# Weights split in two as they land, in place, and a first MLP tile in three passes: banded attention with a rational MLP on one core

## The chip, the core and the metric

One core of a Trainium2 chip runs the whole program. Its engines are TensorE (PE in the profile, its weight loads PEld), VectorE (DVE), ScalarE (ACT), GpSimd (POOL) and SyncE (SP), which here issues every DMA. The metric is the device time of one execution in microseconds (us), the median of three runs.

## The reference

Eight batches of eight heads attend over 576 positions within a window of 128, with a linear bias; the heads are laid side by side to a matrix x of 4608 x 512. Then comes an MLP with a rational activation:

```
scores = where(0 <= i-j < 128, q @ k.T / 8 - slope_h * |i-j|, -1e9)
x      = softmax(scores) @ v                   # 4608 x 512
h      = x @ w_in                              # 4608 x 2048
P      = a0 + a1*h + a2*h^2 + a3*h^3
Q      = 1 + |b0|*|h| + |b1|*h^2
out    = (P / (Q + 1e-6)) @ w_out              # 4608 x 512
```

The weights w_in and w_out are handed to the kernel as 64-bit floating-point numbers of two 32-bit words each.

## The kernel before

**Tiles.** x is cut into 36 blocks of 128 rows and the MLP into 17 tiles: tile 0 has three blocks, tiles 1 to 15 two each, tile 16 three. w_in and w_out are cut into 16 chunks of 128 columns or rows (`c`). For every tile and chunk, "up" (`up`, L625) makes h for the chunk in a PSUM buffer tagged `h` (three of them), ScalarE, GpSimd and VectorE turn it into g (L648 to L666), and "down" (`down`, L681) adds g times w_out into the accumulators `acc`. Tiles of two blocks take two chunks in one step (512 columns), tiles of three one chunk (384 columns). Tile 0's third accumulator takes one of the three `h` buffers.

**Two formats.** From tile 1 on every product is made in three passes of the fast format F32R: the high parts of both factors, high by low and low by high. So x, g and the weights exist as a high and a low part (`x_hi`/`x_lo`, `g_h`/`g_l`, `wi_hi` and `wo_hi`/`w_lo`). Tile 0 runs on whole F32 numbers (`w32`, `x_hi`, `g_32`), which PE does in one, slower, instruction sequence.

**Weights.** Each of the 32 half chunks k (even: w_in, odd: w_out) is loaded by one DMA of 512 KB into a tile `raw_w` and made into F32 by `convert`: GpSimd scales the top words (L582), ScalarE takes three bits of the low words into `cv` in PSUM (L583), and VectorE joins them with two instructions (L584, L585) into `w32`. The first 16 raw tiles have eight homes; of the later ones all even k share one buffer (`x_lo0`) and all odd k one other (`spare`). Later, in `split`, ScalarE rounds `w32` into the high part (L599) and VectorE or GpSimd subtracts it for the low part (L600), which goes to the memory of a `w32` no longer needed.

**Attention.** A unit (`attention`) is a pair of heads for two blocks: scores on PE (L463), masks and exponentials, a GpSimd product (L514), a transposition (L524), two more GpSimd products (L531, L532) and the values (L409). Twelve units belong to the start: six for tile 0, four for tile 1, two that run ahead.

**Order.** `Plan.order()` writes the order of every engine's instructions out by hand beforehand, from due times and costs in ns; the constants `A0` to `BL` set the due times. On the chip each engine then runs its list strictly in that order.

Of the kernel before, what the change touches and what calls it, by code (L numbers as in the profile page):

```python
# [784 lines left out]
```

## Time and profile before

| what | us |
|---|---|
| median of 3 runs (lowest to highest) | 1040.03 (1039.03 to 1040.55) |
| the profiled execution, whole time | 1040.95 |
| the profiled execution, span of the core | 1039.1 |
| PE busy in the span | 1001.4 |
| DVE, ACT, POOL busy | 795.0, 677.0, 524.3 |

The span runs from the first to the last instruction of the core. Busy is the time in which an engine has an instruction under way, waits within an instruction included. PE's clock is given as a share of 2.4 GHz.

### The profile page before, as it was taken

Reading aid. Unit: us, or ns where it says so; the run is one execution under the profiler, and the core shown is the slowest. Engines: PE = TensorE matmul, PEld = TensorE weight load, DVE = VectorE, ACT = ScalarE, POOL = GpSimd, SP = SyncE. Lnnn points to the kernel's source line nnn. Section 1 sums busy time; section 2 is a strip of 40 time slices with the busy share of each in tenths; the row PEclk is TensorE's granted clock in tenths of the full one; section 3 lists DMA queues with packets and bytes.
Section 4 is the critical chain, followed back from the end, with each engine's and each line's share of the span. In section 5 each row is a group of like instructions: output and inputs, shape, how many; then the busy total and the mean of one; then the engine's idle time right before and its main releaser. Section 6 shows DMA issues by size and latency. Waiting matters only on the chain.

```text
span 1039.1 us, 24386 instructions
## 1 busy us (share of the span) xinstructions
PE 1001.4 (96%) x9223; PEld 856.0 (82%) x9223; DVE 795.0 (77%) x1916; ACT 677.0 (65%) x1572; POOL 524.3 (50%) x570
## 2 busy tenths in 40 slices
PE   5899879999999999999999999999999999999998
PEld 4654447888898989898989888888889888898897
DVE  4798789877777777777777777777777786877776
ACT  3766767666766666766666666666665767676664
POOL 2854479455454445444445555545453635465332
PEclk7899999999999999999999999999999999999999
DMA  7945522020212121211212111212121212120000
GB/s 226 293 120 164 177 66 69 27 92 27 92 30 84 35 83 47 61 55 60 62 47 68 48 62 48 68 45 68 52 73 47 67 46 83 31 76 2 21 1 31
DMA packets 75894, 74.15 MB, mean 71 GB/s; under 512 B 7808, under 2 KB 60544, under 8 KB 75776
## 3 DMA queue, kind: packets, MB, share of 16 engines
q1 hardware_dynamic: 75776, 72.58, 22.8%
q8 instruction: 73, 1.20, 0.5%
q14 instruction: 45, 0.37, 0.1%
HBM read 63.11 MB, written 9.44 MB: 70 GB/s over the span
## 4 chain that ended last, share of the span: by engine, by line
PE 86%; DVE 4%; DMA 3%; ACT 2%; SPq 2%; POOL 2%; issue 1%; DVEq 0%; POOLq 0%; ACTq 0%
PE h L625 38%; PE acc L681 37%; PE sc L409 5%; PE sc L463 4%; PE pt L524 3%; DMA raw_w<-in_w_out 2%; SPq L384 1%; ACT o L709 1%; DVE w_lo L600 1%; DMA kq<-in_kqv 1%; DVE h L658 0%; POOL g_q L651 0%; DVE g_q L657 0%; DMA raw_w<-in_w_in 0%; DVE cv L584 0%
## 5 line engine op out<-in xcount | busy, mean ns | idle before, releaser
L625 PE MATMUL h<-x_hi,wi_hi 128*128 128x256 f32 (+1 forms) x1024 | 304.3, 297 | 1.9 <-DVE g L661 1.2
L625 PE MATMUL h<-x_lo,wi_hi 128*128 128x256 f32 (+1 forms) x1024 | 292.3, 285 | 0.0
L625 PE MATMUL h<-x_hi,w_lo 128*128 128x256 f32 (+1 forms) x960 | 273.4, 285 | 0.0
L649 POOL TENSOR_SCALAR g_q<-g_u,babs 128x512 f32<-128x512 f32 (+1 forms) x152 | 115.6, 760 | 257.0 <-ACT g_u L648 194.2
L625 PEld LDWEIGHTS h<-x_lo,wi_hi 128*128 128x128 f32 x1024 | 193.2, 189 | 34.7 <-issue 1.9
L625 PEld LDWEIGHTS h<-x_hi,wi_hi 128*128 128x128 f32 x1024 | 193.5, 189 | 28.2 <-issue 3.1
L681 PE MATMUL acc<-wo_hi,g_h 128*128 128x512 f32 x528 | 209.4, 397 | 1.1
L681 PE MATMUL acc<-wo_hi,g_l 128*128 128x512 f32 x528 | 196.7, 398 | 0.0
L681 PE MATMUL acc<-w_lo,g_h 128*128 128x512 f32 x495 | 195.0, 394 | 0.0
L651 POOL TENSOR_TENSOR g_q<-g_q,g_u 128x512 f32<-128x512 f32 (+1 forms) x152 | 188.1, 1237 | 10.8
L625 PEld LDWEIGHTS h<-x_hi,w_lo 128*128 128x128 f32 x960 | 181.5, 189 | 0.0
L657 DVE SCALAR_TENSOR_TENSOR g_q<-g_q,h 128x512 f32<-128x512 f32 (+1 forms) x152 | 99.8, 656 | 84.9 <-ACT h L656 84.5
L505 ACT ACTIVATE pr<-pr,st 128x128 f32<-128x128 f32 x288 | 114.1, 399 | 67.0 <-DVE st L500 66.7
L514 POOL TENSOR_TENSOR pr<-pr,st 128x512 f32<-128x512 f32 x72 | 76.4, 1060 | 157.3 <-DVE st L513 90.8
L652 DVE TENSOR_TENSOR g_p<-h,g_p 128x512 f32<-128x512 f32 (+1 forms) x152 | 100.6, 662 | 65.0 <-ACT g_p L650 64.9
L654 ACT ACTIVATE g_u<-g_q,guard 128x512 f32<-128x512 f32 (+1 forms) x152 | 106.9, 703 | 62.6 <-POOL g_q L651 62.5
L648 ACT ACTIVATE g_u<-h 128x512 f32<-128x512 f32 (+1 forms) x152 | 87.0, 572 | 72.5 <-PE h L625 72.3
L650 ACT ACTIVATE g_p<-h,na 128x512 f32<-128x512 f32 (+1 forms) x152 | 114.9, 756 | 0.8 <-DVE h L658 0.8
L653 DVE SCALAR_TENSOR_TENSOR g_p<-g_p,na,h 128x512 f32<-128x512 f32 (+1 forms) x152 | 108.7, 715 | 2.6
L658 DVE SCALAR_TENSOR_TENSOR h<-g_p,na,h 128x512 f32<-128x512 f32 (+1 forms) x152 | 109.6, 721 | 0.0
L681 PEld LDWEIGHTS acc<-wo_hi,g_h 128*128 128x128 f32 x528 | 99.2, 188 | 9.1 <-ACT o L709 5.3
L666 DVE TENSOR_TENSOR g_l<-h,g_h 128x512 fp32r<-128x512 f32 (+1 forms) x136 | 91.0, 669 | 13.5 <-ACT g_h L665 13.0
(72 smaller groups left out, 1630.6 us busy)
## 6 DMA issues: line engine op xcount, KB each, us to landing
kq<-in_kqv SPq DMA_DIRECT2D x68, 320.0 KB, 3.1
v<-in_kqv SPq DMA_DIRECT2D x288, 64.0 KB, 2.4
out<-o SPq DMA_DIRECT2D x33, 256.0 KB, 2.0
raw_w<-in_w_in SPq DMA_DIRECT2D x16, 512.0 KB, 4.4
raw_w<-in_w_out SPq DMA_DIRECT2D x16, 512.0 KB, 5.2
bias_t<-in_bias SPq DMA_DIRECT2D x44, 64.0 KB, 2.3
kq<-in_kqv SPq DMA_DIRECT2D x4, 384.0 KB, 3.6
out<-o SPq DMA_DIRECT2D x6, 128.0 KB, 1.8
```

Source lines behind the costliest of these rows:

```text
L505: nc.scalar.activation(ap(pr)[:, :, y, :], ap(pr)[:, :, y, :], AF.Exp, bias=ap(st)[:, y : y + 1], scale=-1.0, accum_out=ap(st)[:, 4 + y : ...
L625: nc.tensor.matmul(h(n), w[:, k, :], x[:, k, :], start=(k == 0 and m == 0), stop=(k == NKC - 1 and m == len(seq) - 1))
L649: plan.op(E, {"g": tsc}, lambda e: nc.gpsimd.tensor_scalar(v(g_q), v(g_u), ap(babs)[:, 1:2], ap(babs)[:, 0:1], ALU.mult, ALU.add), reads=[ ...
L650: plan.op(E, {"a": act(W, 1, 2) - 20}, lambda e: nc.scalar.activation(v(g_p), v(h_s), AF.Identity, bias=ap(na)[:, 2:3], scale=ap(na)[:, 3: ...
L651: plan.op(E, {"g": ttc}, lambda e: nc.gpsimd.tensor_tensor(v(g_q), v(g_q), v(g_u), ALU.mult), reads=[(g_q, 0), (g_u, 0)], writes=[(g_q, 0)])
L652: plan.op(E, {"v": dve(W)}, lambda e: nc.vector.tensor_tensor(v(g_p), v(h_s), v(g_p), ALU.mult), reads=[(h_s, 0), (g_p, 0)], writes=[(g_p, ...
L653: plan.op(E, {"v": dve(W, 1)}, lambda e: stt(v(g_p), v(g_p), ap(na)[:, 1:2], v(h_s), ALU.add, ALU.mult), reads=[(h_s, 0), (g_p, 0)], write ...
L654: plan.op(E, {"a": act(W, 0, 1)}, lambda e: nc.scalar.activation(v(g_u), v(g_q), AF.Ln, bias=guard, scale=1.0), reads=[(g_q, 0)], writes=[ ...
L657: plan.op(E, {"v": dve(W)}, lambda e: stt(v(g_q), v(g_q), GUARD, v(h_s), ALU.add, ALU.mult), reads=[(g_q, 0), (h_s, 0)], writes=[(g_q, 0)])
L658: plan.op(E, {"v": dve(W, 1)}, lambda e: stt(v(h_s), v(g_p), ap(na)[:, 0:1], v(h_s), ALU.add, ALU.mult), reads=[(g_p, 0), (h_s, 0)], write ...
L666: plan.op(E, {"v": dve(W)}, lambda e: nc.vector.tensor_tensor(v(g_l), v(h_s), v(g_h).bitcast(F32), ALU.subtract), reads=[(h_s, 0), (g_h, 0 ...
L681: nc.tensor.matmul(ap(accs[t][i]), x[:, sl], w, start=(c == 0 and part == 0 and m == 0), stop=(c == NFC - 1 and (part == 1 or t == 0) and ...
```

## The change

`convert` now also splits. All of it happens in the raw tile itself: ScalarE scales the top words by a function with two slopes (`Prelu`), which also folds the sign into the number; the three bits of the low words come from ScalarE (`Relu`) in two thirds of the cases and from a shift on VectorE in one third; one VectorE instruction joins them. At once the high part is copied (35% on VectorE, the rest on ScalarE) and the low part subtracted (15% on VectorE, the rest on GpSimd). `split`, `w32` and `cv` go away. Raw tiles 16 to 23 have four homes, those from 24 on three buffers of their own. Tile 0 has `x_lo` and runs in three passes like the others. In the activation, g's high part is written by VectorE straight away and the low part is made from the remainder of the division; the ScalarE copy into `g_h` (L665) and the negated coefficients `na` go away. 5% of the L649 instructions move from GpSimd to VectorE. All due-time constants are new.

```diff
-                plan.op(A + 0.3, {"a": act(P, 1)}, lambda e, b=b: nc.scalar.copy(into(xh)[:, b], src(b)), reads=[sk[b]], writes=[(xh, items[b])])
+                plan.op(A + 0.3, {"a": act(P, 1)}, lambda e, b=b: nc.scalar.copy(into(xh)[:, b], src(b)), writes=[sk[b], (xh, items[b])])
+                plan.op(A + 0.4, {"v": dve(P)}, lambda e, b=b: nc.vector.tensor_sub(into(xl)[:, b], src(b), into(xh)[:, b].bitcast(F32)), reads=[sk[b], (xh, items[b])], writes=[(xl, items[b])])
...
+    def home(k):
+        return 8 + k % 8 if k < 16 else 12 + k % 4 if k < 24 else None
...
+        raw = slot(sb3, [P, 2 * DM], I32, "raw") if m is None else slot(const, [P, 2 * DM], I32, f"raw_w{k}", tag=f"w{m}")
...
-        plan.op(T, {"g": 840}, lambda e: eng[e].tensor_scalar(top().bitcast(F32), top().bitcast(F32), 2.0**-112, 1.0, ALU.mult, ALU.mult), reads=[(raw, 0)], writes=[(raw, 0)])
-        plan.op(T, {"a": 700}, lambda e: nc.scalar.activation(cv(), low().bitcast(U32), AF.Relu, bias=low_bias, scale=2.0**-29), reads=[(raw, 1)], writes=[ck])
-        plan.op(T + 1, {"v": 603}, lambda e: nc.vector.scalar_tensor_tensor(cv(), top(), 3, cv(), ALU.logical_shift_left, ALU.bitwise_or), reads=[(raw, 0), ck], writes=[ck])
-        plan.op(T + 1, {"v": 603}, lambda e: nc.vector.scalar_tensor_tensor(bits().bitcast(I32), top(), -0x80000000, cv(), ALU.bitwise_and, ALU.bitwise_or), reads=[(raw, 0), ck], writes=[(bits_s, k % 2)],
...
+        plan.op(T, {"a": 620}, lambda e: nc.scalar.activation(top().bitcast(F32), top().bitcast(F32), AF.Prelu, scale=2.0**-112, alpha=-(2.0**32)), writes=[(raw, 0)])
+        if share(FS, k):
+            plan.op(T, {"v": 400}, lambda e: nc.vector.tensor_single_scalar(low(), low(), 29, op=ALU.logical_shift_right), writes=[(raw, 1)])
+        else:
+            plan.op(T, {"a": 700}, lambda e: nc.scalar.activation(low(), low().bitcast(U32), AF.Relu, bias=low_bias, scale=2.0**-29), writes=[(raw, 1)])
+        plan.op(T + 1, {"v": 603}, lambda e: nc.vector.scalar_tensor_tensor(low(), top(), 3, low(), ALU.logical_shift_left, ALU.bitwise_or), reads=[(raw, 0)], writes=[(raw, 1)])
...
-        plan.op(T, {"a": 532}, lambda e: nc.scalar.copy(hi(), shape(val())), reads=[(v_s, k % 2)], writes=[(hi_s, c)], after=1000 * (T - SL))
-        plan.op(T + 1, {"v": 603, "g": 1225}, lambda e: eng[e].tensor_tensor(shape(lo()), shape(val()), hi().bitcast(F32), ALU.subtract),
...
+        plan.op(T + 2, {"v": 400} if share(FH, k) else {"a": 620}, lambda e: nc.scalar.copy(hi(), val()) if e == "a" else nc.vector.tensor_copy(hi(), val()), reads=[(raw, 1)], writes=[(hi_s, c)])
+        plan.op(T + 2, {"v": 603} if share(FL, k) else {"g": 1225}, lambda e: eng[e].tensor_tensor(lo(), val(), hi().bitcast(F32), ALU.subtract),
...
-            if t == 0:
-                seq = [(ap(w32[c])[:, 0].rearrange("p (k f) -> p k f", k=NKC), ap(xh))]
...
+            seq = [(w_h, ap(xh)), (w_h, ap(xl)), (w_l, ap(xh))]
...
-        plan.op(E, {"a": act(W, 0)}, lambda e: nc.scalar.activation(v(h_s), v(g_u), AF.Exp, scale=-1.0), reads=[(g_u, 0)], writes=[(h_s, 0)])
-        plan.op(E, {"v": dve(W)}, lambda e: stt(v(g_q), v(g_q), GUARD, v(h_s), ALU.add, ALU.mult), reads=[(g_q, 0), (h_s, 0)], writes=[(g_q, 0)])
-        plan.op(E, {"v": dve(W, 1)}, lambda e: stt(v(h_s), v(g_p), ap(na)[:, 0:1], v(h_s), ALU.add, ALU.mult), reads=[(g_p, 0), (h_s, 0)], writes=[(h_s, 0)])
...
-            plan.op(E, {"v": dve(W)}, lambda e: stt(v(h_s), v(g_q), 2.0, v(h_s), ALU.subtract, ALU.mult), reads=[(h_s, 0), (g_q, 0)], writes=[(h_s, 0)])
-            plan.op(E, {"a": act(W, 1) - 28}, lambda e: nc.scalar.copy(v(g_h), v(h_s)), reads=[(h_s, 0)], writes=[(g_h, 0)])
-            plan.op(E, {"v": dve(W)}, lambda e: nc.vector.tensor_tensor(v(g_l), v(h_s), v(g_h).bitcast(F32), ALU.subtract), reads=[(h_s, 0), (g_h, 0)], writes=[(g_l, 0)])
+        plan.op(E, {"a": act(W, 0)}, lambda e: nc.scalar.activation(v(g_u), v(g_u), AF.Exp, scale=-1.0), reads=[(g_u, 0)], writes=[(g_u, 0)])
+        g_h, g_l = slot(sb3, [P, 512], F32R, "g_h"), slot(sb3, [P, 512], F32R, "g_l")
+        plan.op(E, {"v": dve(W, 1)}, lambda e: stt(v(g_h), v(h_s), ap(ab_sb)[:, 0:1], v(g_u), ALU.add, ALU.mult), reads=[(h_s, 0), (g_u, 0), (ab_sb, 0)], writes=[(g_h, 0)])
+        plan.op(E, {"v": dve(W)}, lambda e: stt(v(g_q), v(g_q), GUARD, v(g_h).bitcast(F32), ALU.add, ALU.mult), reads=[(g_q, 0), (g_h, 0)], writes=[(g_q, 0)])
+        plan.op(E, {"v": dve(W, 1)}, lambda e: stt(v(h_s), v(h_s), ap(ab_sb)[:, 0:1], v(g_q), ALU.add, ALU.subtract), reads=[(h_s, 0), (g_q, 0), (ab_sb, 0)], writes=[(h_s, 0)])
+        plan.op(E, {"v": dve(W)}, lambda e: nc.vector.tensor_tensor(v(g_l), v(h_s), v(g_u), ALU.mult), reads=[(h_s, 0), (g_u, 0)], writes=[(g_l, 0)])
...
-        if t == 1:
-            for k in range(2 * NFC):
-                split(k)
```

## Rows read from the trace of the kernel before

**Rows 1.** The page: the engines' busy time, and the chain of work that ended last, by engine.

```profile
PE 1001.4 (96%) x9223; PEld 856.0 (82%) x9223; DVE 795.0 (77%) x1916; ACT 677.0 (65%) x1572; POOL 524.3 (50%) x570
...
PE 86%; DVE 4%; DMA 3%; ACT 2%; SPq 2%; POOL 2%; issue 1%; DVEq 0%; POOLq 0%; ACTq 0%
```

**Rows 2.** Busy time of each engine in six stretches: tile 0's beginning, tile 0, the passage to tile 1, tile 1, the long middle and the end. Columns: stretch and its length, busy time of each engine with its count of instructions, granted PE clock, DMA share, GB/s.

```profile
core 0: us, PE busy (x) PEld busy (x) DVE busy (x) ACT busy (x) POOL busy (x), PEclk, DMA share, GB/s
0.00:44.70 44.70, 29.77 (x436) 23.23 (x437) 25.23 (x112) 23.17 (x85) 22.10 (x33) 0.73 0.87 270
44.70:135.80 91.10, 82.50 (x386) 43.16 (x384) 75.03 (x159) 62.32 (x131) 48.12 (x64) 1.00 0.51 155
135.80:162.60 26.80, 18.64 (x175) 12.36 (x176) 23.75 (x52) 17.96 (x47) 23.41 (x18) 0.94 0.19 58
162.60:200.00 37.40, 36.74 (x335) 32.83 (x334) 36.00 (x72) 28.04 (x61) 27.78 (x26) 1.00 0.15 47
200.00:1000.00 800.00, 798.93 (x7730) 714.21 (x7729) 609.49 (x1475) 526.32 (x1213) 391.07 (x417) 1.00 0.18 55
1000.00:1039.10 39.10, 34.83 (x170) 30.25 (x168) 25.54 (x49) 19.17 (x40) 11.81 (x14) 0.99 0.06 21
```

**Rows 3.** PE's instructions in order of time, 100 to 163 us: start, duration, engine, line, and in brackets the idle time before and who ended it. A wait within tile 0, and tile 0's last down product.

```profile
119.71 0.91 PE L625 MATMUL h<-x_hi,w 128*128 128x384 f32 x2 [1.40 <-DVE g L661]
...
161.55 1.02 PE L681 MATMUL acc<-w,g 128*128 128x512 f32 x2
```

**Rows 4.** The instructions of SP's queue in order of time, 100 to 125 us: two loads of odd half chunks that follow each other in one buffer.

```profile
109.16 0.33 SPq L579 DMA_DIRECT2D raw_w<-in_w_out  x1
...
115.57 0.33 SPq L579 DMA_DIRECT2D raw_w<-in_w_out  x1
```

**Rows 5.** GpSimd's and VectorE's instructions in order of time, between those two loads.

```profile
112.95 0.66 POOL L582 TENSOR_SCALAR raw_w<-raw_w 128x512 f32<-128x512 f32 x1 [3.54 <-DVE g L661]
...
114.75 0.68 DVE L585 SCALAR_TENSOR_TENSOR w<-raw_w,cv 128x512 int32<-128x512 int32 x1
```

**Rows 6.** The chain that ended last, in order of time: start, duration, what, and how many in a row. The first two are tile 0 (F32, each product two records), the third a tile of two blocks, the last two tile 16, which has three blocks like tile 0 but three passes.

```profile
58.25 1.29 PE h L625 x4
59.54 3.43 PE acc L681 x8
...
208.44 3.95 PE h L625 x33
...
988.57 2.09 PE h L625 x12
...
1021.47 2.08 PE acc L681 x9
```

**Rows 7.** Groups of instructions from 44.7 to 162.6 us: busy time and mean ns of one, then idle time of the engine before them and who ended it.

```profile
L583 ACT ACTIVATE cv<-raw_w,low_bias 128x512 int32<-128x512 uint32 x25 | 18.1, 726 | 5.6 <-DVE w L585 2.9 <-DVE g L661 0.8 <-DMA raw_w<-in_w_out 0.8
...
L585 DVE SCALAR_TENSOR_TENSOR w<-raw_w,cv 128x512 int32<-128x512 int32 x26 | 17.6, 683 | 0.3
L582 POOL TENSOR_SCALAR raw_w<-raw_w 128x512 f32<-128x512 f32 x23 | 15.2, 666 | 25.2 <-DMA raw_w<-in_w_in 8.3 <-DVE g L661 7.5 <-DVE h L658 6.0
...
L599 ACT CAST wi_hi<-w 128x512 fp32r<-128x512 f32 x12 | 7.4, 613 | 0.0
L600 POOL TENSOR_TENSOR w_lo<-w,wo_hi 128x512 fp32r<-128x512 f32 x4 | 6.9, 1724 | 0.0
L599 ACT CAST wo_hi<-w 128x512 fp32r<-128x512 f32 x11 | 6.8, 616 | 0.0
L600 POOL TENSOR_TENSOR w_lo<-w,wi_hi 128x512 fp32r<-128x512 f32 x4 | 6.0, 1510 | 0.9 <-DVE w_spare L600 0.8
...
L600 DVE TENSOR_TENSOR w_lo<-w,wi_hi 128x512 fp32r<-128x512 f32 x5 | 5.6, 1129 | 0.8 <-POOL w_lo L600 0.7
...
L600 DVE TENSOR_TENSOR w_lo<-w,wo_hi 128x512 fp32r<-128x512 f32 x5 | 4.3, 858 | 0.8 <-POOL w_lo L600 0.8
```

**Rows 8.** VectorE's instructions in order of time, 61.6 to 63.6 us: from start to start is what one costs in a dense stretch.

```profile
61.64 0.68 DVE L585 SCALAR_TENSOR_TENSOR w<-raw_w,cv 128x512 int32<-128x512 int32 x1
62.24 0.55 DVE L652 TENSOR_TENSOR g_p<-h,g_p 128x384 f32<-128x384 f32 x1
62.71 0.35 DVE L512 TENSOR_TENSOR st<-st,tiny 128x4 f32<-128x4 f32 x1
62.98 0.60 DVE L653 SCALAR_TENSOR_TENSOR g_p<-g_p,na,h 128x384 f32<-128x384 f32 x1
```

**Rows 9.** Groups from 0 to 44.7 us, VectorE: two small instructions of four columns, the first with two inputs in SBUF, the second with one.

```profile
L512 DVE TENSOR_TENSOR st<-st,tiny 128x4 f32<-128x4 f32 x7 | 2.7, 383 | 1.3 <-ACT pr L505 1.1
...
L513 DVE RECIPROCAL st<-st 128x4 f32<-128x4 f32 x7 | 1.2, 171 | 0.1
```

**Rows 10.** Instructions of GpSimd and VectorE that overlap, in order of time: one pair early, one in the passage to tile 1.

```profile
18.97 1.04 POOL L514 TENSOR_TENSOR pr<-pr,st 128x512 f32<-128x512 f32 x1
...
19.25 0.79 DVE L318 TENSOR_SCALAR na<-ab_sb 128x4 f32<-128x4 f32 x1 [2.67 <-DMA ab_sb<-in_ab]
...
140.38 1.27 POOL L600 TENSOR_TENSOR w_lo<-w,wi_hi 128x512 fp32r<-128x512 f32 x1 [0.80 <-DVE w_spare L600]
...
140.75 1.45 DVE L600 TENSOR_TENSOR w_lo<-w,wo_hi 128x512 fp32r<-128x512 f32 x1
```

**Rows 11.** The page's groups, whole span: loads of function tables on ScalarE.

```profile
L293 ACT ACT_TABLE_LOAD x1 | 1.3, 1283 | 0.7 <-PEq L773 0.7
```

More of the change, by code (lines that the diff above doesn't have):

```diff
@@ L285, in ap, with share @@
         return s.ap
+    def share(part, i):
+        return int((i + 1) * part) > int(i * part)
     def act(n, psum, ptr=0):
@@ L299, in banded_attention_ratio_mlp @@
     ab_sb = slot(const, [P, 6], F32, "ab_sb")
-    na = slot(const, [P, 4], F32, "na")
     babs = slot(const, [P, 2], F32, "babs")
@@ L431, in out_values @@
         plan.op(A + 0.4, {"v": dve(2 * P)}, lambda e: nc.vector.tensor_sub(into(xl), src(), into(xh).bitcast(F32)),
-                reads=sk + [(xh, k) for k in items], writes=[(xl, k) for k in items], follows=[raws[k] for k in range(16, 2 * NFC, 2)] if t == 2 else ())
+                reads=sk + [(xh, k) for k in items], writes=[(xl, k) for k in items])
     def attention(u):
@@ new lines, in convert @@
+        plan.op(T - WL, {"s": 1456}, load, writes=[(raw, 0), (raw, 1)], after=1000 * (T - WL - 4), follows=before)
+        plan.op(T, {"a": 620}, lambda e: nc.scalar.activation(top().bitcast(F32), top().bitcast(F32), AF.Prelu, scale=2.0**-112, alpha=-(2.0**32)), writes=[(raw, 0)])
[3 more added lines that the diff above has]
+            plan.op(T, {"a": 700}, lambda e: nc.scalar.activation(low(), low().bitcast(U32), AF.Relu, bias=low_bias, scale=2.0**-29), writes=[(raw, 1)])
@@ L648, in mlp @@
         plan.op(E, {"a": act(W, 1)}, lambda e: nc.scalar.activation(v(g_u), v(h_s), AF.Abs), reads=[(h_s, 0)], writes=[(g_u, 0)])
-        plan.op(E, {"g": tsc}, lambda e: nc.gpsimd.tensor_scalar(v(g_q), v(g_u), ap(babs)[:, 1:2], ap(babs)[:, 0:1], ALU.mult, ALU.add), reads=[(g_u, 0), (babs, 0)], writes=[(g_q, 0)])
-        plan.op(E, {"a": act(W, 1, 2) - 20}, lambda e: nc.scalar.activation(v(g_p), v(h_s), AF.Identity, bias=ap(na)[:, 2:3], scale=ap(na)[:, 3:4]), reads=[(h_s, 0), (na, 0)], writes=[(g_p, 0)])
+        plan.op(E, {"v": 160 + 0.55 * W} if share(FQ, 8 * t + cs[0] // 2) else {"g": tsc}, lambda e: eng[e].tensor_scalar(v(g_q), v(g_u), ap(babs)[:, 1:2], ap(babs)[:, 0:1], ALU.mult, ALU.add), reads=[(g_u, 0), (babs, 0)], writes=[(g_q, 0)])
@@ L686, in mlp @@
             last = c == NFC - 1
-            for part in range(1 if t == 0 else 2):
+            for part in range(2):
                 for i in range(nb):
-                    r = [(w32[c], 1), (g_h, 0)] if t == 0 else [(wo_hi, c), (w_lo[c], 1), (g_h, 0)] if part == 0 else [(wo_hi, c), (g_l, 0)]
+                    r = [(wo_hi, c), (w_lo[c], 1), (g_h, 0)] if part == 0 else [(wo_hi, c), (g_l, 0)]
                     if last and end and part == 1:
```

98 lines of the change are left out of this document (34 added, 64 removed).

## The prediction, made blind

> **What bounds the kernel now.** I read the page first. PE is busy for 1001.4 us of the 1039.1 us span and holds 86% of the chain that ended last [rows 1], so the time is PE's work plus PE's idle time: 1001.4 + 37.7, and 1.85 us around the span in the profiled execution (1040.95 - 1039.1). Its whole time is 0.9 above the median of the runs; I take that off at the end.
>
> The table by stretches shows where the 37.7 lie [rows 2]. From 200 to 1000 us PE works 798.93 of 800: nothing done on another engine can help there. The end (39.1 - 34.83 = 4.3) is the last down products' way out. The rest is the start: 14.9 idle before 44.7 us, 8.6 in tile 0, 8.2 in the passage to tile 1, and 0.7 to 200 us. With 0.7, 1.1 and 4.3 the three last stretches hold 6.0, which I leave as they are.
>
> What holds PE in tile 0? PE's order of time names VectorE's release of the h buffers [rows 3]. Behind that stands a load loop. For k from 16 on, all odd half chunks share one buffer: its loads are issued 6.4 us apart [rows 4]; the first lands after 3.8 us, when GpSimd's L582 can run (3.54 us idle before it), and the join at 114.75 frees the buffer at 115.4 [rows 5]. L582 stands in GpSimd's strict order ahead of the activation's products, so a late load holds up g as well. So a chunk of tile 0 takes at least 6.4 us in this part, though PE needs less. Then comes the passage: the subtractions of `split` fill GpSimd, and tile 0's last down product ends only at 162.6 [rows 3].
>
> **The change part by part: PE.** Tile 0 costs now, per chunk, 2 x 1.29 up and three quarters of 3.43 down, 5.15 us; tile 16, with the same shape in three passes, takes 2.09 + 2.08 = 4.17 [rows 6]. Saved: 16 x 0.98 = 15.7 us. PE's work becomes 985.7. That becomes time only as far as PE's idle time doesn't grow, so the question is how long the stretch that now runs from 44.7 to 162.6 us (117.9 us) will be. PE's work in it is 82.5 + 18.6 = 101.1 [rows 2]; after, 85.4, and some work of tile 1 that can slip in ahead: between none and two steps of two chunks, 24 products of 0.12 us each [rows 6]; I take one, 2.9. Sum 88.3.
>
> **The load loop.** The two single buffers go. In the new loop a buffer waits for the load (3.8), a scaling, an extraction, a join, a copy and a subtraction, some 0.7 + 0.7 + 0.7 + 0.6 [rows 7] and 1.3 for an undisturbed subtraction (its row comes below), 7.8 us, over four buffers for k of 16 to 23 and three after: 3.9 and 5.2 us a chunk plus handovers. That is below what follows for VectorE, so the loop no longer sets the pace; without the fourth buffer it would be near.
>
> **VectorE in that stretch.** Busy now 75.0 + 23.8 = 98.8 [rows 2]. Removed: the second join, 26 x 0.60 (start to start [rows 8]) = 15.6; the ten subtractions shown, 9.9 [rows 7]. Added: 26 half chunks are left to convert, a third with a shift and 35% with a copy, 17.8 instructions of 512 columns with one source. No row has one; the bounds are 0.17 (four columns [rows 9]) and 0.60 (512 columns, two sources); I take the middle, 0.4: 7.1. Subtractions left to VectorE, 3.8 x 0.6 = 2.3. In the activation, tile 0 goes from five instructions to six a chunk, 16 x 0.53 (0.60 less the overlap of 0.08 [rows 8]) = 8.5. Sum 98.8 - 25.5 + 17.9 = 91.2.
>
> To that come waits. A VectorE instruction with two inputs in SBUF waits for a GpSimd instruction under way: the subtraction issued at 140.75 ends 0.55 after GpSimd's of 140.38 has ended, and a four-column product with one input, at 19.25, ends just with GpSimd's [rows 10]. On average the four-column addition loses 0.383 - 0.171 = 0.21 us early on [rows 9], the subtraction 0.99 - 0.68 = 0.31 in the passage [rows 7]. The old joins have one input in PSUM and lose nothing (0.683 [rows 7]). The new ones have both in SBUF, as has the new product for g_q. I count 26 joins, 18 shifts and copies, 4 subtractions, 16 products and 5 small additions: 69 instructions x 0.21 = 14.5 (bounds 0 and 69 x 0.31 = 21.4). I take 0.21 since GpSimd's load doesn't rise: 71.5 busy now, less 15.2 for L582 and 12.9 for eight subtractions, plus 26 x 0.85 x 1.27 = 28.1 makes 71.5.
>
> The page "SBUF — State Buffer" of the Trainium skill, section "Who interferes with whom", states this as an exclusive lock and extends it to single-source copies and scalar instructions in a two-port mode. By that rule the shift and the copy take part at full width, which only the four-column row bears out; without them the waits would be 51 x 0.21 and the sum below 4 us less, 1025.
>
> VectorE: 91.2 + 14.5 = 105.7. When it had most to do it was busy 36.0 of 37.4 us, 96% [rows 2]. So the stretch becomes 105.7 / 0.96 = 110.1 us instead of 117.9, and PE is idle in it for 110.1 - 88.3 = 21.8 instead of 16.8.
>
> **The rest, hidden.** ScalarE: 80.3 busy now, less nine extractions (6.3) and 3.8 of copies, plus 26 scalings of at most 0.73: 89 of 110 us; covered, and a bound if VectorE were faster. The first stretch: six half chunks get their subtraction before 44.7, and tile 0 twelve small ones for x_lo, while GpSimd and VectorE are busy 22.1 and 25.2 of 44.7 [rows 2]; I take nothing (up to 4 us if the first chunk's low part is late). `cv` leaves PSUM, so attention's bank is freer: covered by VectorE. Per chunk pair of the later tiles a ScalarE copy goes away and one more VectorE instruction has two SBUF inputs: PE's 798.93 of 800 covers both, VectorE having 190 us free there; uncovered, 122 x 0.31 = 38 us. DMAs are the same 32 loads, earlier; their share in tile 0 is 0.51 [rows 2]. The new order moves everything, at no cost I can read.
>
> **Sum.** PE 985.7, idle 14.9 + 21.8 + 6.0 = 42.7, and 1.85: 1030.2 against the profiled 1040.95; less 0.9, **1029 us**.
>
> **Rivals.**
> - *VectorE is no bound, PE is.* Its waits vanish in idle time and the shift is cheap (17.8 x 0.2): 91.2 - 3.6 = 87.6, less than PE's 88.3. At the 91% that PE had in tile 0 (82.5 of 91.1) the stretch lasts 97.0, idle 8.7: 1016; at 96%, 1011. For: the load loop was the one strict pace. Against: ScalarE would need 89 of 97 us.
> - *GpSimd and VectorE block each other: slower.* The joins come in the middle of each conversion, every copy and subtraction waits for them, and the activation's GpSimd products queue behind 1.27 us subtractions. The change turns to a loss when the stretch is longer than 120.8 us: VectorE 116.0, so 24.8 us of waits, 0.36 per instruction. Seen are 0.21 and 0.31. At 0.45 (over a third of 1.27) it's 69 x 0.45 = 31.1, a stretch of 127.4, 1046. For: the same pattern stretched GpSimd's subtractions to 1.5 and 1.7 us [rows 7].
> - *Table loads: much slower.* If Prelu isn't in the loaded set of functions, each scaling brings a load of 1.28 us [rows 11] before and after it: 52 x 1.28 = 67 us more on ScalarE in that stretch, 156 us, idle 68: 1075. Against: one load serves Relu, Abs, Identity, Exp and Ln in the whole trace [rows 11]; Prelu isn't among what ran. The page "ScalarE: Activation LUTs" of the Trainium skill, section "Table sets: the hidden batching unit", says that a function outside the active set costs such a load and that cheap functions are in every set; the row agrees with its 1283 ns, and for Prelu nothing here shows it.
> - *Half of it:* waits at 0.31 and the first chunk 4 us late: stretch 117.3, 1040, no change.
>
> **Chances.** The forecast (1021 to 1035, waits 0.1 to 0.29) 0.5; PE-bound (1010 to 1021) 0.2; between the forecast and a loss (1035 to 1042) 0.15, half of it within 0.2% of before, about what a measurement of this kernel can tell; blocking (above 1042) 0.12; tables 0.03. So faster 0.77, same 0.08, slower 0.15. The range leaves out the lowest part of the second case and the last two: 1012 to 1041.
>
> **What would show it.** PE's busy time falls to about 986; tile 0 shows three-pass products at 0.17 us; loads of half chunks no longer come 6.4 us apart from one buffer; tile 0's last down product ends near 155; joins of tile 0 last some 0.9 us where GpSimd runs and 0.68 elsewhere; the stretch from 200 us on is unchanged. The prediction is wrong if tile 0's last down ends before 142 or after 165, if PE idles in the long middle, or if the table load count is above one.

## The result: slower, 1046.5 us

The changed kernel takes 1046.53 us (median of four runs, 1046.11 to 1048.9) where the kernel before took 1040.18 on the same chip: a ratio of 1.0068, interval 1.005 to 1.0085. The forecast was 1029 and its range ended at 1041; the measured time is that of the rival in which GpSimd and VectorE block each other. The profiled execution took 1046.46, 1.86 of it around the span.

The page of the changed kernel: busy time, and the chain of work that ended last, by engine.

```profile
PE 995.5 (95%) x9339; PEld 888.4 (85%) x9339; DVE 825.2 (79%) x1924; ACT 619.8 (59%) x1447; POOL 528.9 (51%) x546
...
PE 83%; DVE 7%; ACT 3%; issue 2%; POOL 2%; DMA 2%; SPq 1%; DVEq 0%; ACTq 0%; POOLq 0%
```

PE's work fell by 5.9 us against [rows 1], not by 15.7, and its idle time grew from 37.7 to 1044.6 - 995.5 = 49.1. The stretches, with the columns of [rows 2], show both in one place.

```profile
0.00:44.70 44.70, 27.62 (x403) 21.74 (x403) 27.36 (x118) 26.94 (x94) 23.00 (x27) 0.75 0.86 253
44.70:140.00 95.30, 71.60 (x516) 59.58 (x516) 89.18 (x171) 72.36 (x156) 74.66 (x63) 0.86 0.52 164
140.00:167.00 27.00, 23.75 (x157) 20.21 (x157) 16.83 (x33) 9.29 (x18) 10.01 (x12) 0.91 0.08 22
167.00:200.00 33.00, 32.23 (x303) 28.83 (x302) 23.16 (x54) 19.27 (x43) 15.26 (x16) 1.00 0.15 46
200.00:1000.00 800.00, 799.92 (x7769) 722.76 (x7768) 635.24 (x1494) 472.34 (x1101) 389.79 (x412) 1.00 0.19 55
1000.00:1044.60 44.60, 40.40 (x197) 35.24 (x195) 33.38 (x60) 19.60 (x38) 16.17 (x18) 0.98 0.05 18
```

From 44.7 to 140 us VectorE is busy 94% of the time and PE 75%, at a granted clock of 0.86 where [rows 2] had 1.00. From 140 to 167 VectorE falls to 62%, and tile 0 still isn't done. From 200 to 1000 PE works without a gap, as before.

The groups of VectorE between 44.7 and 170 us show what fills it (joins L579, g_q's product L645, copies L588, shifts L576):

```profile
L579 DVE SCALAR_TENSOR_TENSOR raw_w<-raw_w 128x512 int32<-128x512 int32 x18 | 18.0, 1011 | 1.4 <-ACT raw_w L578 1.4
L645 DVE SCALAR_TENSOR_TENSOR g_q<-g_q,g_h 128x384 f32<-128x384 f32 x16 | 14.4, 901 | 0.3
...
L579 DVE SCALAR_TENSOR_TENSOR raw<-raw 128x512 int32<-128x512 int32 x8 | 8.5, 1068 | 0.1
...
L588 DVE CAST wo_hi<-raw_w 128x512 fp32r<-128x512 f32 x4 | 3.9, 962 | 0.0
...
L576 DVE TENSOR_SCALAR raw<-raw 128x512 int32<-128x512 int32 x3 | 3.2, 1074 | 0.0
```

What such an instruction lasts alone, and what it waits for, stands in the instructions in order of time, first VectorE's, then GpSimd's, of the same 15 us:

```profile
86.79 1.78 DVE L579 SCALAR_TENSOR_TENSOR raw_w<-raw_w 128x512 int32<-128x512 int32 x1
...
89.48 1.60 DVE L645 SCALAR_TENSOR_TENSOR g_q<-g_q,g_h 128x384 f32<-128x384 f32 x1
...
96.92 0.56 DVE L645 SCALAR_TENSOR_TENSOR g_q<-g_q,g_h 128x384 f32<-128x384 f32 x1
97.39 0.69 DVE L579 SCALAR_TENSOR_TENSOR raw_w<-raw_w 128x512 int32<-128x512 int32 x1
...
98.52 0.41 DVE L588 CAST wo_hi<-raw_w 128x512 fp32r<-128x512 f32 x1
...
100.91 1.04 DVE L588 CAST wo_hi<-raw_w 128x512 fp32r<-128x512 f32 x1
...
86.54 1.48 POOL L589 TENSOR_TENSOR w_lo<-raw_w,wi_hi 128x512 fp32r<-128x512 f32 x1
88.00 1.10 POOL L636 TENSOR_SCALAR g_q<-g_u,babs 128x384 f32<-128x384 f32 x1
89.36 1.31 POOL L589 TENSOR_TENSOR w_lo<-raw_w,wi_hi 128x512 fp32r<-128x512 f32 x1 [0.25 <-ACT wi_hi L588]
...
97.51 1.10 POOL L636 TENSOR_SCALAR g_q<-g_u,babs 128x384 f32<-128x384 f32 x1 [3.75 <-ACT g_u L635]
...
99.77 1.90 POOL L589 TENSOR_TENSOR w_lo<-raw_w,wo_hi 128x512 fp32r<-128x512 f32 x1
```

The join of 86.79 ends at 88.57, 0.55 after GpSimd's subtraction (86.54 + 1.48 = 88.02); g_q's product of 89.48 ends 0.41 after the subtraction of 89.36. The same two last 0.69 and 0.56 when they come first. The copy of 98.52 takes 0.41; the one of 100.91, issued while a subtraction is under way, ends 0.28 after it. The other way round, GpSimd's one-input product of 97.51 waits for the join of 97.39 and takes 1.10 instead of 0.66.

### The profile page after: what moved, and what is told of

It reads as the page before. It is cut to its first block, busy times and chain, and to the rows that moved or that the text cites. A ratio compares the mean times of both kernels' runs of the same rounds, so it can differ in the third digit from the quotient of the medians.

```text
span 1044.6 us, 24297 instructions
## 1 busy us (share of the span) xinstructions
PE 995.5 (95%) x9339; PEld 888.4 (85%) x9339; DVE 825.2 (79%) x1924; ACT 619.8 (59%) x1447; POOL 528.9 (51%) x546
## 4 chain that ended last, share of the span: by engine, by line
PE 83%; DVE 7%; ACT 3%; issue 2%; POOL 2%; DMA 2%; SPq 1%; DVEq 0%; ACTq 0%; POOLq 0%
PE h L611 37%; PE acc L659 35%; PE sc L411 5%; PE sc L466 4%; PE pt L527 3%; DVE raw_w L579 1%; DVE g_q L645 1%; DVE g_h L644 1%; POOL w_lo L589 1%; DVE h L646 1%; POOL g_q L638 1%; ACT pr L508 1%; DMA bias_first<-in_bias 1%; DMA raw_w<-in_w_in 0%; DVE raw L579 0%
## 5 line engine op out<-in xcount | busy, mean ns | idle before, releaser
L611 PE MATMUL h<-x_hi,wi_hi 128*128 128x256 f32 (+1 forms) x1084 | 324.4, 299 | 11.2 <-DVE g_l L647 11.1
L611 PE MATMUL h<-x_lo,wi_hi 128*128 128x256 f32 (+1 forms) x1084 | 313.5, 289 | 0.0
L611 PE MATMUL h<-x_hi,w_lo 128*128 128x256 f32 (+1 forms) x1084 | 312.8, 289 | 0.0
L659 PE MATMUL acc<-wo_hi,g_h 128*128 128x512 f32 x576 | 230.1, 399 | 12.2 <-DVE g_h L644 12.2
L659 PE MATMUL acc<-w_lo,g_h 128*128 128x512 f32 x576 | 229.9, 399 | 0.0
L611 PEld LDWEIGHTS h<-x_hi,w_lo 128*128 128x128 f32 x1084 | 205.7, 190 | 0.0
L644 DVE SCALAR_TENSOR_TENSOR g_h<-h,ab_sb,g_u 128x512 fp32r<-128x512 f32 (+1 forms) x152 | 109.4, 720 | 116.9 <-ACT g_u L642 116.1
L635 ACT ACTIVATE g_u<-h 128x512 f32<-128x512 f32 (+1 forms) x152 | 87.2, 574 | 138.6 <-PE h L611 123.8
L645 DVE SCALAR_TENSOR_TENSOR g_q<-g_q,g_h 128x512 f32<-128x512 f32 (+1 forms) x152 | 110.0, 724 | 9.2
L637 ACT ACTIVATE g_p<-h,ab_sb 128x512 f32<-128x512 f32 (+1 forms) x152 | 114.0, 751 | 4.1 <-PE h L611 4.1
L646 DVE SCALAR_TENSOR_TENSOR h<-h,ab_sb,g_q 128x512 f32<-128x512 f32 (+1 forms) x152 | 110.5, 727 | 2.3
L640 DVE SCALAR_TENSOR_TENSOR h<-g_p,ab_sb,h 128x512 f32<-128x512 f32 (+1 forms) x152 | 109.7, 721 | 3.3 <-ACT g_u L635 1.1
```

The costliest lines, as they stand in the source:

```text
L611: nc.tensor.matmul(h(n), w[:, k, :], x[:, k, :], start=(k == 0 and m == 0), stop=(k == NKC - 1 and m == len(seq) - 1))
L637: plan.op(E, {"a": act(W, 1, 2) - 20}, lambda e: nc.scalar.activation(v(g_p), v(h_s), AF.Identity, bias=ap(ab_sb)[:, 2:3], scale=ap(ab_sb) ...
L640: plan.op(E, {"v": dve(W, 1)}, lambda e: stt(v(h_s), v(g_p), ap(ab_sb)[:, 1:2], v(h_s), ALU.add, ALU.mult), reads=[(h_s, 0), (g_p, 0), (ab ...
L644: plan.op(E, {"v": dve(W, 1)}, lambda e: stt(v(g_h), v(h_s), ap(ab_sb)[:, 0:1], v(g_u), ALU.add, ALU.mult), reads=[(h_s, 0), (g_u, 0), (ab ...
L645: plan.op(E, {"v": dve(W)}, lambda e: stt(v(g_q), v(g_q), GUARD, v(g_h).bitcast(F32), ALU.add, ALU.mult), reads=[(g_q, 0), (g_h, 0)], writ ...
L646: plan.op(E, {"v": dve(W, 1)}, lambda e: stt(v(h_s), v(h_s), ap(ab_sb)[:, 0:1], v(g_q), ALU.add, ALU.subtract), reads=[(h_s, 0), (g_q, 0), ...
```

## The experiments

Three theories: (1) VectorE and GpSimd wait for each other; (2) PE's gaps lower its clock, and that sets the end; (3) the chain of each chunk (two h buffers) and the order of the due times do. Ratios below are to the kernel before, measured on the same chip; us taken off are against the changed kernel's 1046.53, and the kernel before, measured anew with each group of runs, stayed within 1039.87 and 1040.53. Every edit but two made the plan write out another order; those two keep it and are named. FS, FH and FL are the shares of shifts, copies and subtractions that stand on VectorE (0.33, 0.35 and 0.15 in the changed kernel), CO and L0 two of the due-time constants. "Abs" is ScalarE's first instruction of a chunk's activation (L635), which shows when the chunk's up products are done; groups and means are from 44.7 to 170 us where nothing else is said.

**Joins fed from PSUM.** FS = 0, and the extraction writes `cv` in PSUM as before (tags acc and sc); the join reads it.

```
-    activation(low(), low().bitcast(U32), AF.Relu, ...), writes=[(raw, 1)]
+    activation(cv(), low().bitcast(U32), AF.Relu, ...), reads=[(raw, 1)], writes=[ck]
-    scalar_tensor_tensor(low(), top(), 3, low(), ...)
+    scalar_tensor_tensor(low(), top(), 3, cv(), ...), reads=[(raw, 0), ck]
```

> One part undone: the joins get their low bits from PSUM again (as in the kernel before) and all extractions stand on ScalarE, so no join has two inputs in SBUF and no shift runs on VectorE; copies, subtractions and the rest stay as in the changed kernel. Theory 1 (VectorE and GpSimd block each other): joins in tile 0 fall from 1.0 to about 0.68 us, VectorE loses some 16 us of work and waits before 140 us, ScalarE gains 9 x 0.7 = 6; tile 0's last down product ends 5 to 12 us earlier, the time is 1034 to 1041. Theory 2 (PE's idle gaps lower its clock, and the lower clock sets the end): the clock in tile 0 stays near 0.87 and the time near 1044 to 1047. Theory 3 (two h buffers and a longer activation chain set the pace of tile 0's chunks, 5.6 us each even when the other engines are free): joins do get shorter, but VectorE's saved time turns into idle time and the time is 1042 to 1047.

Measured: 1039.86 (ratio 0.9998, 0.9987 to 1.001), in theory 1's range. Only its time is used; how long its joins last is not shown.

**Products of zeros in tile 0** (order kept).

```
+    def fill(count):
+        for _ in range(count):
+            nc.tensor.matmul(ap(accs[0][0]), zero(P), zero(512), start=False, stop=False)
...
+            if t == 0 and k == 0 and c >= 4: fill(3)      # in up
+            if t == 0 and i == 0 and part == 0 and c >= 1: fill(4)      # in down
```

> Nothing is taken away: in tile 0, TensorE gets products of zeros added to the accumulator (four ahead of each chunk's first down product, three ahead of the up products of chunks 4 to 15; 96 in all, about 0.22 us each at full clock, 21 us), placed where it waited, and the plan's order is the same. Theory 2 (the lower clock sets the end): the granted clock between 48 and 170 us rises from 0.87 to about 1.00, the real products of tile 0 lose some 9 us, and the time falls to 1037 to 1043. Theories 1 and 3 (VectorE's waits, or the chain of each chunk, set the pace and TensorE only follows): the clock rises the same, the products get shorter, TensorE waits longer instead, and the time is 1044 to 1049.

Measured: 1051.43 (1.0103, 1.0087 to 1.012). Two windows of this kernel:

```profile
80.00:100.00 20.00, 16.97 (x130) 14.11 (x129) 19.33 (x41) 12.84 (x30) 13.84 (x13) 1.00 0.79 263
100.00:120.00 20.00, 15.77 (x75) 13.15 (x74) 19.89 (x31) 15.77 (x31) 15.96 (x12) 1.00 0.52 161
```

The changed kernel, same windows:

```profile
80.00:100.00 20.00, 16.32 (x111) 13.11 (x111) 19.05 (x40) 14.71 (x33) 13.32 (x13) 0.83 0.74 246
100.00:120.00 20.00, 13.23 (x56) 10.87 (x54) 19.90 (x27) 13.95 (x27) 18.23 (x12) 0.91 0.52 161
```

The time is above both ranges. The clock is 1.00 in these windows for 0.83 and 0.91 (from 48 to 170 us it rose only from 0.88 to 0.93, not to 1.00), and yet the ten chunks from the first (Abs at 54.68) to the eleventh (134.14) take 79.5 us, in the changed kernel 79.4 (51.03 to 130.44). So the lower clock doesn't set the pace there. The first Abs comes 3.7 us later in this execution, but the first product of zeros runs at 69.90 us, so that isn't their doing, and its cause stays open. Behind the eleventh chunk the last Abs comes 32.9 us later, 30.0 in the changed kernel, with the clock at 1.00 from 140 to 167 us: there PE's products stand in the way, and the zeros among them.

**h released early.** In tile 0 the second VectorE product writes g_p, and the rest reads g_p.

```
-    stt(v(h_s), v(g_p), ap(ab_sb)[:, 1:2], v(h_s), ...)
+    stt(v(y_s), v(g_p), ap(ab_sb)[:, 1:2], v(h_s), ...)      # y_s = g_p if t == 0 else h_s; read as y_s below
```

> In tile 0 alone, the activation's second VectorE product writes to SBUF (g_p) instead of back to h, and the four instructions behind it read g_p, so an h buffer in PSUM comes free after the second VectorE instruction of the chain and not after the last; three more VectorE instructions a chunk then have two inputs in SBUF. Theory 3 (two h buffers and the chain from up products to g_l set 5.6 us a chunk): the pace falls to about 4 us (g_u's two buffers, 8 us from Abs to g_l), tile 0's last down ends 5 to 10 us earlier, the time is 1036 to 1042. Theory 1 (blocking): 48 more instructions that can wait for GpSimd, 0.2 to 0.45 us each, 10 to 20 us more on a VectorE that is 95% busy: 1046 to 1058.

Measured: 1046.72 (1.0063, 1.0048 to 1.0078), no change against the changed kernel. The three instructions that now have two SBUF inputs went from 0.61, 0.61 and 0.55 us to 1.06, 0.95 and 0.84, and VectorE is busy 18.9 us of 140 to 160 instead of 11.2: the freed buffer brought no time while the waits grew. On theory 3's buffers this run decides nothing.

**All subtractions on VectorE.** FL = 1.0 for 0.1467.

> All subtractions of the weights stand on VectorE (0.15 of them before), so GpSimd keeps only the activation's and the attention's instructions. Theory 1: joins, shifts and copies on VectorE fall to 0.7 and 0.4 us and the activation's GpSimd products no longer queue behind 1.3 us subtractions; VectorE gets 22 x 0.6 = 13 us of work and loses some 16 us of waits: 1038 to 1045. Theory 3: the chain of each chunk gets VectorE's added work in front of it and gains what GpSimd's queue held up: 1043 to 1050. Theory 2: the clock goes with TensorE's gaps, whatever VectorE does: near 1046 unless the gaps shrink.

Measured: 1035.19 (0.9954, 0.9939 to 0.9969): 11 us off, better than any theory had it. Joins on raw 0.68 us, on raw_w 0.82, shifts 0.42 to 0.43; the clock 0.98 between 44.7 and 140. The order is another too, and what that is worth shows further down.

**GpSimd keeps its subtractions, nothing of the conversion on VectorE waits for them.** Joins from PSUM (tag ptx for k from 4 on), FS = FH = 0.

> GpSimd keeps its subtractions (0.85 of them). What could wait for them on VectorE goes: the joins get their low bits from PSUM (a bank of ptx for k from 4 on), and shifts and copies stand on ScalarE. Theory 1a (what cost the time is VectorE's waits for GpSimd in joins, shifts and copies): as good as the run with all subtractions on VectorE, 1033 to 1038. Theory 1b (what cost the time is GpSimd's 1.3 to 1.8 us subtractions in front of the activation's products): the joins get short (0.68 us), but the chunks of tile 0 stay slow and the time is 1040 to 1046. If ScalarE, with some 12 us more, becomes the bound: it is over 90% busy between 60 and 140 us.

Measured: 1031.26 (0.9912, 0.9897 to 0.9927), 15 us off and below the range of theory 1a. The groups of this kernel, 0 to 170 us:

```profile
L585 DVE SCALAR_TENSOR_TENSOR raw_w<-raw_w,cv 128x512 int32<-128x512 int32 x24 | 16.4, 683 | 4.6 <-ACT cv L584 4.5
L595 POOL TENSOR_TENSOR w_lo<-raw_w,wo_hi 128x512 fp32r<-128x512 f32 x11 | 15.0, 1367 | 12.6 <-ACT wo_hi L594 12.6
```

The subtractions are still on GpSimd, and the joins last 0.68. That speaks for VectorE's waits as the cost and against the place that the subtractions take in GpSimd's queue. Not all of the 15 us are waits: shifts and copies left VectorE too (8 and 10 from 44.7 to 170 us, 7.5 us at 0.42 and 0.415), and the order is another. ScalarE is 90% busy from 60 to 140 us (18.74 + 19.41 + 16.56 + 17.54 of 80) and is near the bound.

**All subtractions on VectorE, shifts and copies on ScalarE.** FL = 1.0, FS = FH = 0.

> All subtractions on VectorE, as in the run of that name, and shifts and copies on ScalarE. VectorE was 99% busy between 60 and 140 us in that run; it gets 17 instructions of 0.42 us less, 7 us, and ScalarE 17 of some 0.7 us more, 12 us on 75 of 95. If VectorE's work alone sets the stretch: 1028 to 1033. If the chain of each chunk (two h buffers, 5.6 us) does: 1034 to 1037.

Measured: 1029.19 (0.9889, 0.9874 to 0.9904).

```profile
44.70:140.00 95.30, 76.42 (x566) 62.87 (x565) 92.87 (x198) 86.11 (x178) 43.19 (x42) 1.00 0.55 168
```

The time is in the range for VectorE's work. VectorE is 97% busy, and 7 us less work on it gave 6 us. In the profiled execution, which took 1026.75, PE's clock is 1.00 with no product added, and its work over the span is 981.8 us.

**The old activation** in all tiles; split and three passes stay.

> One part undone: the activation of the kernel before (low part by a ScalarE copy and a subtraction, no product with two inputs in SBUF), in all tiles; the split and the three passes in tile 0 stay. Theory 1 (blocking): the g_q product in tile 0 falls from 0.90 to 0.56 us, 5 us less on VectorE; 1040 to 1045. Theory 3 (the chain of each chunk sets the pace): g_h comes two VectorE products and a copy later, about 1.7 us, g_l about 0.5 us later; 1047 to 1052.

Measured: 1043.55 (1.0025, 1.0015 to 1.0034): 3 us off, within theory 1's range. g_q's product takes 0.55; the joins stay at 0.99 and 1.01.

**Joins from PSUM and all subtractions on VectorE.** FL = 1.0, FS = 0, `cv` in ptx.

> All subtractions on VectorE, joins with low bits from PSUM, no shift on VectorE, copies shared as in the changed kernel. The joins on raw_w fall from 0.82 to 0.68 us (2.6 us in 19) and eight shifts of 0.42 go (3.4), so VectorE has 6 us less than in the run with all subtractions on it. If VectorE's work sets the stretch: 1028 to 1033. If the chain of each chunk does: 1034 to 1037. If the one bank of ptx holds up attention's transposes or ScalarE (6 us more) becomes the bound: above 1037.

Measured: 1036.37 (0.9968, 0.9953 to 0.9983). The time is in the range that was given for the chain of each chunk (theory 3). The joins fell to 0.68, but tile 1's first up products ran from 122.80 us on, ahead of tile 0's last three chunks, and tile 0's last four came 12.5, 13.2, 4.9 and 6.8 us apart: the gain seems lost in the order. Which of the single bank and the due times did it, was not tried.

**One due time later.** CO = 30.0 for 21.554.

> The changed kernel with one due time other: the conversions of the odd half chunks (output weights) are due 8.4 us later (30.0 for 21.554), all work as it was. Theory 3/order (conversions are done too early, fill VectorE until 140 us and leave it half idle until 167 us, while tile 0's last chunks wait): VectorE's work is spread further, tile 0's last down ends 4 to 8 us earlier, 1038 to 1043. Theory 1 (the waits between VectorE and GpSimd make VectorE's work, and the sum of the work sets the end): the same number of waits, 1044 to 1049.

Measured: 1040.16 (1.0, 0.9991 to 1.001): 6.4 us off, with the waits about as before (joins 1.11 and 1.02 us, 1.01 and 1.07 in the changed kernel; g_q's product 0.73 for 0.90). So the order is a loss of its own. Where it lies (window 140 to 167 us of this kernel, to be held against 23.75, 16.83 and 0.91 above):

```profile
140.00:167.00 27.00, 25.62 (x185) 22.09 (x183) 21.37 (x46) 14.58 (x32) 13.09 (x14) 1.00 0.09 28
```

**Half of the subtractions on each.** FL = 0.5, FS = FH = 0.

> Half of the subtractions on VectorE, half on GpSimd (0.15 on VectorE in the changed kernel), shifts and copies all on ScalarE, as in the run that had all subtractions on VectorE (1029). VectorE gets 11 subtractions of 0.7 to 0.9 us less than in that run, 9 us, and the joins and g_q products wait again for 11 to 13 GpSimd subtractions. If a GpSimd subtraction costs VectorE in waits as much as doing it there (26 joins from 0.7 to 1.0 over 22 subtractions, 0.4 us, with g_q's 0.25 x 16 / 22 = 0.2): about as much as it saves, 1027 to 1031. If the waits are worth more: above 1031. If GpSimd's share is free: 1020 to 1026.

Measured: 1034.68 (0.9942, 0.9924 to 0.996), 5.5 us above the run with all on VectorE: in these two orders a subtraction on GpSimd cost more than it saved. Joins 0.88 and 0.78, g_q's product 0.84.

**The new activation alone**, in tiles 1 to 16 of the kernel before.

> One part alone: the kernel before, with the new activation in tiles 1 to 16 (tile 0, the load of the weights, their split and the due times as before). The long middle is PE's; expected the same as before within 0.3%, 1038 to 1042, if the activation's part of the change costs nothing outside tile 0. If its product with two SBUF inputs costs there: VectorE above 700 of 800 us between 200 and 1000 and a longer time.

Measured: 1042.33 (1.0017, 1.0007 to 1.0027). That is 2.1 us slower, clear of the interval and just above the range. VectorE is busy 637 of 800 us from 200 to 1000, and PE 796.4 of 800, 798.9 before; in the changed kernel PE has 799.92 there, so the changed kernel doesn't carry these 2 us.

**All subtractions on VectorE, tile 0 taken to last longer.** FL = 1.0, FS = FH = 0, and L0 = 92.955 for 83.48.

> As the run with all subtractions on VectorE and the rest on ScalarE (1029), and one due time as in the kernel before: tile 0 is taken to last 92.955 and not 83.48, so its chunks, tile 1 and what follows are due later against the conversions. If the order costs time there (its last chunk's up products came 12 us after the one before, behind tile 1's first): 1025 to 1028. If VectorE's work is all: 1028 to 1031.

Measured: 1026.86 (0.9868, 0.9849 to 0.9887). Tile 0's last Abs comes at 141.07, 7.2 us after the one before; without the edit it came at 143.97, 12.0 after.

**GpSimd's subtraction with one input** (order kept).

```
-    eng[e].tensor_tensor(lo(), val(), hi().bitcast(F32), ALU.subtract)
+    nc.vector.tensor_tensor(lo(), val(), hi().bitcast(F32), ALU.subtract) if e == "v" else
+    nc.gpsimd.tensor_scalar(lo(), val(), 2.0**-14, 0.0, ALU.mult, ALU.add)
```

> The changed kernel, in the same order on every engine, with GpSimd's 28 subtractions of the weights replaced by a product of one SBUF input with a constant (this leaves out the difference: the low part of those weights isn't computed). GpSimd's instruction gets shorter (a one-input product of 512 columns took 0.66 in the kernel before) and has one input in SBUF where it had two; all that VectorE and ScalarE run is as in the changed kernel. Theory 1 (VectorE waits for GpSimd's two-input instructions): joins in tile 0 fall from 1.0 towards 0.7 us, shifts and copies from 0.83 towards 0.42, and the time falls by 8 to 14, to 1032 to 1038. Theory 3/order alone: VectorE's instructions get shorter, but the end comes from the order: 1040 to 1045. If one-input instructions of GpSimd hold VectorE up as well: joins stay above 0.9 us and 1042 to 1047.

Measured: 1037.66 (0.9975, 0.9964 to 0.9986), 8.9 us off with not one instruction of VectorE, ScalarE, PE or the loads moved, at the upper end of theory 1's range. This kernel leaves out the low part of those weights. Groups of this kernel, 44.7 to 170 us:

```profile
L579 DVE SCALAR_TENSOR_TENSOR raw_w<-raw_w 128x512 int32<-128x512 int32 x18 | 15.3, 858 | 1.0 <-ACT raw_w L578 0.9
L589 POOL TENSOR_SCALAR w_lo<-raw_w 128x512 fp32r<-128x512 f32 x17 | 14.3, 839 | 1.4
...
L589 POOL TENSOR_SCALAR w_lo<-raw 128x512 fp32r<-128x512 f32 x7 | 7.6, 1080 | 7.0 <-DVE raw L579 5.7 <-DVE w_lo L589 1.0
L579 DVE SCALAR_TENSOR_TENSOR raw<-raw 128x512 int32<-128x512 int32 x8 | 6.9, 862 | 0.1
```

Joins fall from 1.01 and 1.07 to 0.86, half of the way to 0.68. A GpSimd instruction with one input holds VectorE up too, only for less long, as a join and a product of this kernel show:

```profile
81.58 1.05 DVE L579 SCALAR_TENSOR_TENSOR raw_w<-raw_w 128x512 int32<-128x512 int32 x1
...
81.44 0.65 POOL L589 TENSOR_SCALAR w_lo<-raw_w 128x512 fp32r<-128x512 f32 x1
```

The join ends 0.54 us after the product. The edit makes GpSimd's queue shorter as well, but little of the gain can come that way: from 44.7 to 140 us none of VectorE's waits between its instructions names GpSimd in either kernel, and ScalarE's waits for GpSimd's g_q fall only from 4.8 to 3.2 us. VectorE's busy time from 44.7 to 140 falls from 89.18 to 83.91, and tile 1's first up product comes at 156.04 instead of 165.14 us, 9.1 earlier, as the end does.

**All subtractions on GpSimd.** FL = 0.

> The last four subtractions that the changed kernel has on VectorE go to GpSimd as well (0.15 on VectorE before, 0 now). VectorE gets 4 x 0.68 = 2.7 us less work, and four more GpSimd instructions of 1.3 to 1.8 us that it can wait for. Theory 1 with the price that the run with half of them gave (each subtraction on GpSimd costs more than on VectorE): 1047 to 1051. If VectorE's own work decides: 1043 to 1046.

Measured: 1039.85 (0.9998, 0.9988 to 1.0008), which neither had. The joins are as long as before (1.04 and 0.94), but the order is another: tile 1's first up product comes at 157.37 us, 7.8 earlier, ahead of tile 0's last Abs (157.56) and not 4.7 behind it (160.47). Most of the 6.7 us would then be the order's, as in the run with the later due time; VectorE's 2.7 us less work is in them too, and the two were not taken apart. It also means that runs which differ in order carry some 6 us of it, so the price per subtraction from the run with half of them is not firm.

**Later due time on top of the best.** FL = 1.0, FS = FH = 0, L0 = 92.955, CO = 30.0.

> All subtractions on VectorE, shifts and copies on ScalarE, tile 0 taken to last 92.955 (1027), and in addition the odd half chunks' conversions due at 30.0 and not 21.554, the edit that took 6 us off the changed kernel. If order and waits are two separate losses: 1020 to 1025. If the later due time only moved VectorE's waits about in the changed kernel: 1026 to 1030.

Measured: 1024.11 (0.9853, 0.9838 to 0.9868), the fastest of all, 15.8 us below the kernel before and 22 below the changed one. The due time gave 2.7 here and 6.4 in the changed kernel, so waits and order are two losses that overlap in part.

## Why the prediction was wrong, point by point

The forecast for the profiled execution was 1030.2; it took 1046.5. The 16.2 us are 9.8 of PE's work (995.5 for 985.7) and 6.4 of its idle time (49.1 for 42.7). As stretches: tile 0's last down ends at 167.2, "near 155" was forecast, and behind 165 was a sign of being wrong.

- **VectorE's waits, the term that was mis-sized.** The count was right, 69 instructions, and the price wasn't. Against 0.68 for a join, 0.555 for g_q's product, 0.415 for a copy, 0.42 for a shift and 0.17 for a small addition, the groups from 44.7 to 170 us lose 8.8 + 5.5 + 4.4 + 3.1 + 0.5 = 22.3 us, 0.32 an instruction; 14.5 at 0.21 was taken, 0.31 was the bound, and the rival needed 0.36. The 0.21 came from a four-column addition in a stretch where GpSimd was half idle [rows 9]. The 0.21 was taken "since GpSimd's load doesn't rise" from 71.5 us; it rose to 84.7 (74.66 + 10.01), in part since GpSimd waits as well. In tile 0 it is 78% busy (74.66 of 95.3), its subtractions last 1.3 us and more, and each conversion puts a join and a copy beside a subtraction. Of the 26 joins 14 were held up, and each of them ends 0.55 or 0.56 us after the GpSimd instruction that held it. That these waits cost time is shown by the run with one-input products: 8.9 us in the same order.
- **The stretch as VectorE's work over 0.96, the step that failed.** VectorE's sum came out as forecast, 106.0 from 44.7 to 167 us (89.18 + 16.83) for 105.7, but by luck: the waits were 7.8 above and the undisturbed work 7.5 below. And 106.0 took 122.3 us, 87%. The share of 96% came from a stretch of [rows 2] with much independent work. Here VectorE is 94% busy until 140 us, doing conversions ahead of need, and then only 62%, since what is left are four chunks, in which PE's products and the activation, a chain over ScalarE and VectorE, wait for each other by turns. ScalarE's and VectorE's rows of the changed kernel show the chain, PE's where the products of two chunks begin and end:

```profile
145.81 0.49 ACT L635 ACTIVATE g_u<-h 128x384 f32<-128x384 f32 x1 [5.87 <-PE h L611]
...
146.90 0.56 DVE L639 TENSOR_TENSOR g_p<-h,g_p 128x384 f32<-128x384 f32 x1 [3.48 <-ACT g_p L637]
...
150.23 0.62 DVE L644 SCALAR_TENSOR_TENSOR g_h<-h,ab_sb,g_u 128x384 fp32r<-128x384 f32 x1 [2.12 <-ACT g_u L642]
...
140.95 0.69 PE L611 MATMUL h<-x_hi,wi_hi 128*128 128x384 f32 x1 [0.54 <-DVE g_l L647]
...
148.92 0.34 PE L611 MATMUL h<-x_hi,w_lo 128*128 128x384 f32 x1
...
153.83 0.44 PE L611 MATMUL h<-x_hi,wi_hi 128*128 128x384 f32 x1 [0.36 <-DVE g_l L647]
...
160.10 0.33 PE L611 MATMUL h<-x_hi,w_lo 128*128 128x384 f32 x1
```

Tile 0's Abs of 145.81 and 149.29 are followed by those of 156.94 and 160.47, 11.1 us for two chunks: 6.6 us of PE's products of two chunks (153.83 to 160.43) and 4.5 us in which the activation must first give g_l (149.29 to 153.83), and in which PE has attention and down products to do, but no up products of tile 0. So VectorE's sum of work doesn't set this part at all; PE is 88% busy in it. "The new order moves everything, at no cost I can read" was wrong: with the waits left in, one due time alone takes 6.4 us off.
- **PE's work, right at full clock only.** In the run with all subtractions on VectorE and the rest on ScalarE the clock is 1.00 in tile 0 and PE's work 981.8, 3.9 below the forecast. In the changed kernel the clock isn't 1.00:

```profile
59.35 0.66 PE L659 MATMUL acc<-wo_hi,g_h 128*128 128x512 f32 x1 [3.13 <-DVE g_h L644]
59.81 0.63 PE L659 MATMUL acc<-w_lo,g_h 128*128 128x512 f32 x1
...
146.13 0.39 PE L659 MATMUL acc<-wo_hi,g_h 128*128 128x512 f32 x1
```

  After 3.13 us without work a product takes 0.63 us, the lower level of 1.2 GHz, and 0.39 later at 2.4. The prediction took the clock as 1.00, as it had been. The lower one adds to PE's busy time, but the run with products of zeros shows that the pace of tile 0's first eleven chunks doesn't hang on it. In the tail after 140 us it costs 1.7 us: the same products of two chunks last 8.3 us from 140.95 to 149.26, where those before 144.8 ran at the lower level, and 6.6 from 153.83 to 160.43.
- **The load loop: right.** Loads of half chunks from k = 16 on no longer follow each other 6.4 us apart, and of PE's 27 us of idle time from 44.7 to 167 us 22.5 name VectorE (11.4 for g_h, 11.1 for g_l). With the loop gone VectorE was the next bound, as forecast.
- **The first stretch: 2.2 us worse.** PE does 27.62 us of work in it, 29.77 before, and tile 0's first Abs comes at 51.03 us, at 46.96 before; taken as nothing, with up to 4 as the bound. Part of it may be the execution's own: in the run with products of zeros, the first of them at 69.90 us, it came at 54.68.
- **Shift and copy at 0.4 us: right alone** (0.42 and 0.41), 0.80 and 0.85 on average in tile 0. The section "Who interferes with whom" of the page "SBUF — State Buffer" in the Trainium skill counts them among the instructions that can enter a two-port mode and then take part in the lock, and the copy of 100.91 us above agrees with it at 1.04.
- **Long middle, table loads: right.** PE 799.92 of 800, and one table load of 1283 ns as in [rows 11].

Of the cases, the blocking rival (0.12) had the mechanism, and the time in part by luck: its price was 0.45 an instruction for 0.32 measured, and the tail made up for it. The prediction's last rival, waits of 0.31 and a late first chunk, gave 1040, the time of the two kernels with such waits and another order (1040.16 and 1039.85); that fits a loss of 6.5 us by the order, and isn't shown further.

## What to carry to other kernels

When a change puts a second SBUF input or a 512-column copy on VectorE beside a busy GpSimd, price each at a third of a microsecond and more, taken from GpSimd's load in that stretch and not from a quiet one, and ask whether all of it on VectorE isn't cheaper than sharing. A stretch is an engine's work over its busy share only while there is independent work for it: look for a tail in which single chains are left, and which order leads into it. A planner's order is a cost of its own; here one due time was worth as much as the whole loss, so an edit that changes the order can't be priced closer than that unless the order is kept.
